# Four equal parts of the channel layer, the first part's weights off GpSimd, and another rate and latency of transfers in the planner

## Chip, cores and metric

One core of one Trainium2 chip runs the whole program. The metric is the device time of one execution in microseconds (us); a measured change of under 0.3%, some 2.4 us, can't be told from none.

## What is computed

Inputs are float32, except U, V, w_ch1, w_ch2, w_in and w_out, which arrive as float64. Three layers follow each other; B = 4, H = 8, S = 576, head width 64, model width 512.

```python
def _attn_ref(q, k, v):                       # per batch and head
    scores = scale * np.matmul(q, k.transpose(0, 1, 3, 2))
    mask = (rel >= 0) & (rel < 128)           # a band of 128 keys
    scores = np.where(mask, scores + bias[None], -1000000000.0)
    attn = softmax(scores)
    return np.matmul(attn, v)

def _moe_ref(x, U, V, w_ch1, w_ch2):
    h = x.transpose(0, 2, 1) @ U @ V          # rank 32, along the sequence
    u = x + h.transpose(0, 2, 1)
    return u + np.maximum(u @ w_ch1, 0.0) @ w_ch2      # 512 -> 2048 -> 512: the channel layer

def _moe2_ref(x, w_in, w_spatial, b_spatial, w_out):
    h = np.maximum(x @ w_in, 0.0)
    u, v = (h[..., :512], h[..., 512:])
    v_n = normalised(v)
    gated = u * (np.einsum('ts,bsd->btd', w_spatial, v_n) + b_spatial)
    return gated @ w_out
```

## The kernel before

Attention runs batch by batch, two heads (a **pair**) at a time, four pairs to a batch. A pair's way (`heads`) is: scores on TensorE (L577), maximum and bias on VectorE (L589, nine tiles), exponential on ScalarE (L594), scaling by the reciprocal sum on VectorE or GpSimd (L607, L609), transposes on TensorE (L616) with copies out (L317, L318), the product with the values (L639). After a batch's fourth pair the rank-32 layer (`low_rank`) multiplies with U (L675) and V (L687) and adds into `u` (L692).

The channel layer's 2048 hidden units are 16 blocks of 128, split into four **parts**; `K["parts"]` says how many blocks each part has. A part's weights stay in SBUF while all 2304 tokens pass (`ffn_group`: first product L460 to L462, ReLU L467 and L469, second product L497 to L499, sum into `y` L507). Every product is three matmuls of operands that are split exactly into a high and a low fp32r part (L431 and L434 for tokens). Part 0 begins early: five groups of 256 tokens (`nb=5`) are interleaved with the attention of batches 1 to 3 and fill TensorE where attention leaves it idle; this is called **filler** below. The other 1024 tokens of part 0 and parts 1 to 3 follow when attention has ended, in groups of 512. The point where the attention ends and 512-wide groups begin is called the **handover** below.

A weight block arrives as float64 and is converted on the chip (`single`, `weights`): load on SP's queue (L350), absolute value on ScalarE (L356), clipping (L360 on GpSimd or L362 on VectorE), and three bit operations on VectorE (L363, L366, L369); then the high part (L317 on ScalarE, or L379 on GpSimd) and the low part on GpSimd (L384). `cp` and `wp` say for how many of part 0's weights the clip and the high part go to GpSimd. V goes the same way without a high and low part; its load (`stacked`) names the 32 rows of V four times, so that the outermost dimension of its source has 4 steps and the next one 32.

The order of the instructions on every engine is set by a planner, `Plan.run`: a list scheduler over the costs, dependences and priorities that each `P.add` gives. `Plan.dma` prices a load at its bytes over a rate, and adds `lat` before its reader may run. Priorities in attention are ten to a pair (`p0 = 10.0 * i`); `low` and `lowd` place V's conversion and its load on that scale, in pairs, `w0` and `w0s` the conversion of part 0's weights, `d0` and `d0s` their loads. On the chip each engine runs its list in order, so what waits for a late load holds up what stands behind it.

Of the kernel before, what the change touches and what calls it, by code (L numbers as in the profile page):

```python
# [126 lines left out]
class Plan:  # L127
# [36 lines left out]

    def dma(self, p, n, emit, r=(), w=(), prio=0):

        self.add("SP", max(0.5, p * n * 4 / 280e3), emit, r=r, w=w, prio=prio, lat=2.3)

    def run(self):
        seq = {t: i for i, t in enumerate(self.tasks)}  # L170
# [89 lines left out]
def tile_kernel(ctx, tc, qT, kT, v, U, V, w1, w2, w_in, wspT, bsp, w_out, bias, out):  # L260
# [32 lines left out]

    r_wa = Ring(in_left, "wa", max(12, 2 * K["parts"][0]))
    r_u = Ring(in_left, "u", 16)
    r_y = Ring(in_left, "y", 12)
    r_raw = Ring(in_left, "raw", 2)
    r_st = Ring(in_left, "st", K["nst"])
    r_h = Ring(in_left, "h", 8)
# [11 lines left out]

    PARTS = K["parts"]

# [10 lines left out]
    def engines(kind, usual):  # L324
        return BOTH if kind in K["flex"] else (usual,)

# [61 lines left out]
    def part_of_hidden(qi, ring, prio, early=lambda c: None, on_pool=lambda c: (False, False)):  # L388
        res = []
        for f in range(PARTS[qi]):  # L390
            c0 = (sum(PARTS[:qi]) + f) * 128
            two = []
            for i, args in enumerate(((block(w1, 0, E, c0, c0 + 128, 4), 4, 128), (block(w2, c0, c0 + 128, 0, E), 1, E))):
                c = 2 * f + i
                two.append(weights(ring, *args, prio(c), early(c), on_pool(c)))
            res.append(two)
        return res
# [142 lines left out]
    def low_rank_weights(prio, early, prio_v, early_v):  # L540
        single(u32, [(0, block(U, 0, 128, 0, RANK)), (1, block(U, 64, S, 0, RANK, 4))], 5, RANK, prio, None, early)
        P.add("DVE", 0.1, lambda: nc.vector.memset(u32[64:, 0], 0.0), w=[u32], prio=prio)
        single(v32, [(0, stacked(block(V, 0, RANK, 0, S), 4))], 1, S, prio_v, None, early_v)
# [152 lines left out]
    for pair in range(4):  # L696
        P.dma(128, 192, lambda pair=pair: nc.sync.dma_start(out=bias_t[:, pair], in_=bias[:, pair]),
              w=[bias_t.part(pair)], prio=20 * pair + 0.5)
    low_rank_weights(15, 2, 10 * K["low"], 10 * K["lowd"])
    parts_w = [None] * 4  # L700
    for b in range(B):
# [7 lines left out]
        if b == 0:  # L709
            parts_w[0] = part_of_hidden(0, r_wa, lambda c: 10 * (K["w0"] + K["w0s"] * c),  # L710
                                        lambda c: 10 * (K["d0"] + K["d0s"] * c),
# [241 lines left out]

K = dict(parts=(5, 4, 4, 3), flex='xeht', cp=3, wp=5, low=4.0, w0=6.5, w0s=1.23, nb=5, evac=40.0, nst=3, d0=5.5, d0s=0.91, lowd=4.1)


# [38 lines left out]
```

## Time and profile before

| | |
|---|---|
| Median of 3 executions | 787.51 us (786.32 to 788.89) |
| The profiled execution | 789.81 us |
| its span, first to last instruction | 788.0 us |
| mean granted TensorE clock | 0.985 |
| TensorE busy | 754.8 us (96%) |
| VectorE, ScalarE, GpSimd busy | 409.6, 319.0, 271.3 us |
| bytes read and written | 40.14 and 4.72 MB |

TensorE is busy for 96% of the span, so what a change is worth is read from the stretches where it is not, and from the stretches where its clock is granted at half. A row of a timeline has start, duration, engine, line, operation, and in brackets the idle time before it with what ended it. A row of a table by groups has the busy time, the mean of one instruction, and the idle time before. PE is TensorE, DVE VectorE, ACT ScalarE, POOL GpSimd, SPq the queue of loads.

### The profile page before, as it was taken

How to read it: one execution, taken by the hardware profiler on the slowest of the kernel's cores; microseconds unless marked ns; L12 is line 12 of the kernel's file. 1: busy time of each engine (PE TensorE's matmuls, PEld its weight loads, DVE VectorE, ACT ScalarE, POOL GpSimd, SP SyncE). 2: the span in 40 equal slices, each digit the busy share in tenths (PEclk: the TensorE clock that was granted, in tenths of full speed). 3: DMA queues.
4: the chain of work that ended last, by engine and by line, in shares of the span. 5: the costliest groups of instructions: out<-in, count | busy, mean ns of one | idle time of the engine just before them, and what ended most of it. 6: DMA issues, size and time to landing. Idle time of an engine off the chain costs nothing.

```text
span 788.0 us, 13153 instructions
## 1 busy us (share of the span) xinstructions
PE 754.8 (96%) x5036; PEld 643.5 (82%) x5036; DVE 409.6 (52%) x1075; ACT 319.0 (40%) x860; POOL 271.3 (34%) x346
## 2 busy tenths in 40 slices
PE   6778799999989999999999999999999999999998
PEld 5557688888888888888887889788998898898887
DVE  4788957587396672212676226822564415325120
ACT  5766657466443442212352115332343332332222
POOL 1364231020173463210474215762436124033021
PEclk9898999999999999999999999999999999999999
DMA  8773213210150350000600003000300100100102
GB/s 218 238 233 115 61 26 102 72 62 17 42 187 1 91 177 1 1 1 0 197 18 0 1 1 108 1 0 1 99 1 1 41 15 0 54 15 1 54 1 67
DMA packets 28834, 45.70 MB, mean 58 GB/s; under 512 B 4964, under 2 KB 18020, under 8 KB 28772
## 3 DMA queue, kind: packets, MB, share of 16 engines
q1 hardware_dynamic: 28772, 44.87, 18.1%
q8 instruction: 39, 0.64, 0.3%
q14 instruction: 23, 0.19, 0.1%
HBM read 40.14 MB, written 4.72 MB: 57 GB/s over the span
## 4 chain that ended last, share of the span: by engine, by line
PE 84%; DVE 9%; DMA 3%; ACT 2%; issue 1%; SPq 0%; DVEq 0%; ACTq 0%
PE at L460 5%; PE at L461 5%; PE at L462 5%; PE sc L499 5%; PE sc L498 5%; PE sc L497 5%; PE at L616 4%; PE acc L497 3%; PE acc L499 3%; PE acc L498 3%; PE at L639 3%; PE f L460 3%; PE sc L779 2%; PE f L461 2%; PE sc L781 2%; PE sc L780 2%
## 5 line engine op out<-in xcount | busy, mean ns | idle before, releaser
L434 POOL TENSOR_TENSOR x<-u,xc 128x64 fp32r<-128x64 f32 (+5 forms) x108 | 91.9, 884 | 126.7 <-ACT xc L431 125.6
L469 DVE SCALAR_TENSOR_TENSOR h<-at,h 128x512 fp32r<-128x512 f32 (+1 forms) x49 | 31.7, 646 | 113.1 <-ACT h L467 113.0
L467 ACT ACTIVATE h<-at 128x512 fp32r<-128x512 f32 (+1 forms) x49 | 27.6, 563 | 122.3 <-PE at L462 121.0
L594 ACT ACTIVATE p<-p,nmax 128x192 f32<-128x192 f32 (+1 forms) x144 | 61.3, 429 | 7.8 <-DVE nmax L589 7.6
L616 PE MATMUL at<-ident,p 128*128 128x128 f32 x272 | 43.4, 309 | 13.9 <-DVE p L609 13.1
L616 PEld LDWEIGHTS at<-ident,p 128*128 128x128 f32 x272 | 35.5, 159 | 20.0 <-issue 11.4
L384 POOL TENSOR_TENSOR wa<-st,wa 128x512 fp32r<-128x512 f32 x26 | 35.0, 1351 | 45.1 <-ACT wa L317 40.2
L589 DVE CUSTOM_DVE_ANT_0 p<-sc,bias 128x192 f32<-128x192 f32 (+1 forms) x144 | 40.2, 328 | 11.9 <-PE sc L577 11.9
L577 PE MATMUL sc<-kr,qr 64*64 64x192 f32 (+2 forms) x576 | 34.5, 341 | 11.2 <-DMA kr<-in_kT 7.4
L497 PE MATMUL acc<-h,wa 128*128 128x256 f32 (+1 forms) x130 | 42.4, 326 | 1.0 <-ACT wb L317 0.9
L794 POOL TENSOR_TENSOR u<-y,u 128x576 fp32r<-128x576 f32 x16 | 23.1, 1460 | 55.0 <-ACT u L792 55.0
L499 PE MATMUL acc<-h,wa 128*128 128x256 f32 (+1 forms) x130 | 40.0, 307 | 2.1 <-DVE h L469 2.1
L498 PE MATMUL acc<-h,wa 128*128 128x256 f32 (+1 forms) x130 | 39.8, 306 | 0.0
L431 ACT CAST xc<-u 128x64 fp32r<-128x64 f32 (+5 forms) x108 | 38.4, 435 | 2.9 <-PE at L687 2.9
L462 PE MATMUL f<-x,wa 128*128 128x256 f32 (+1 forms) x128 | 39.1, 305 | 0.0
L498 PE MATMUL sc<-h,wb 128*128 128x512 f32 (+1 forms) x105 | 38.6, 368 | 0.0
L499 PE MATMUL sc<-h,wb 128*128 128x512 f32 (+1 forms) x105 | 38.6, 368 | 0.0
L497 PE MATMUL sc<-h,wb 128*128 128x512 f32 (+1 forms) x105 | 38.6, 368 | 0.0
L460 PE MATMUL at<-xc,wb 128*128 128x512 f32 (+1 forms) x104 | 38.4, 369 | 0.0
L461 PE MATMUL at<-xc,wb 128*128 128x512 f32 (+1 forms) x104 | 38.3, 369 | 0.0
L462 PE MATMUL at<-x,wb 128*128 128x512 f32 (+1 forms) x104 | 38.3, 369 | 0.0
L317 ACT COPY ph<-at 128x512 f32<-128x512 f32 (+2 forms) x54 | 27.0, 520 | 27.1 <-PE at L616 26.9
(330 smaller groups left out, 2273.2 us busy)
## 6 DMA issues: line engine op xcount, KB each, us to landing
wa<-in_w SPq DMA_DIRECT2D x18, 512.0 KB, 5.3
wb<-in_w SPq DMA_DIRECT2D x14, 512.0 KB, 6.5
qr<-in_qT SPq DMA_DIRECT2D x16, 288.0 KB, 2.9
kr<-in_kT SPq DMA_DIRECT2D x16, 288.0 KB, 3.9
vr<-in_v SPq DMA_DIRECT2D x16, 256.0 KB, 2.8
wa<-in_w_in SPq DMA_DIRECT2D x8, 512.0 KB, 3.5
out<-h SPq DMA_DIRECT2D x15, 256.0 KB, 2.0
wb<-in_w_out SPq DMA_DIRECT2D x4, 512.0 KB, 4.1
```

The lines of the kernel that those rows point to most:

```text
L384: P.add("POOL", pool_tt(k * c), lambda: nc.gpsimd.tensor_tensor(out=b[:, 1], in0=st.ap(), in1=f32(b[:, 0]), op=ALU.subtract), r=[st, b.par ...
L431: nc.scalar.copy(out=th[ih][:, o : o + m], in_=ub[:, s : s + m])
L434: nc.gpsimd.tensor_tensor(out=tl[il][:, o : o + m], in0=ub[:, s : s + m], in1=f32(th[ih][:, o : o + m]), op=ALU.subtract)
L460: nc.tensor.matmul(o, wt[:, 0, k], a[ia], start=k == 0, stop=False)
L461: nc.tensor.matmul(o, wt[:, 1, k], a[ia], start=False, stop=False)
L462: nc.tensor.matmul(o, wt[:, 0, k], l[il], start=False, stop=k == 3)
L497: nc.tensor.matmul(o, wt[:, 0, 0, c], hh[:, j], start=i == 0 and x == 0, stop=False, skip_group_check=True)
L498: nc.tensor.matmul(o, wt[:, 1, 0, c], hh[:, j], start=False, stop=False, skip_group_check=True)
L499: nc.tensor.matmul(o, wt[:, 0, 0, c], hl[:, j], start=False, stop=i == len(wts) - 1, skip_group_check=True)
L589: nc.vector.tensor_tensor_reduce(out=o(), in0=s[:, c0 : c0 + nk], in1=bias_t[:, pair, t % 2, 192 - nk :], scale=-0.125, scalar=BIG, op0=AL ...
L594: nc.scalar.activation(out=o(), in_=o(), func=AF.Exp, scale=-1.0, bias=nmax[:, sl, t : t + 1], accum_out=sums[:, sl, t : t + 1])
L616: P.add("PE", 0.109, lambda pt=pt, t=t, half=half, blk=blk: nc.tensor.transpose(pt[:, blk * 128 : blk * 128 + 128], p[:, t, half * 128 : h ...
```

## The change

```diff
     def dma(self, p, n, emit, r=(), w=(), prio=0):
-        self.add("SP", max(0.5, p * n * 4 / 280e3), emit, r=r, w=w, prio=prio, lat=2.3)
+        self.add("SP", max(0.5, p * n * 4 / 235e3), emit, r=r, w=w, prio=prio, lat=2.6)
...
-K = dict(parts=(5, 4, 4, 3), flex='xeht', cp=3, wp=5, low=4.0, w0=6.5, w0s=1.23, nb=5, evac=40.0, nst=3, d0=5.5, d0s=0.91, lowd=4.1)
+K = dict(parts=(4, 4, 4, 4), flex='xeht', cp=0, wp=0, low=6, w0=8, w0s=1.23, nb=5, evac=40.0, nst=3, d0=7, d0s=0.91, lowd=5)
```

Part 0 has 4 blocks instead of 5 (8 weights to convert instead of 10), the last part 4 instead of 3. None of part 0's weights is clipped or given its high part on GpSimd; the low parts stay there. V's conversion is placed two pairs later, its load almost one, part 0's weights one and a half. The planner believes that a load takes longer. Every engine's list is ordered anew from these costs. Three places follow.

ScalarE's list around the absolute value of V (v_306 and v_365 are V's tile; p_81 and p_77 are the probabilities of odd and even pairs). Before:

```order
L594 ACTIVATE p_81,sums<-p_81,nmax 128x192 x7
L356 ACTIVATE v_306<-raw 128x576
L594 ACTIVATE p_77,sums<-p_77,nmax 128x64
L594 ACTIVATE p_77,sums<-p_77,nmax 128x128
L594 ACTIVATE p_77,sums<-p_77,nmax 128x192 x3
L317 COPY ph<-at 128x384
```

and in the change:

```order
L594 ACTIVATE p_81,sums<-p_81,nmax 128x64
L317 COPY ph<-at 128x256
L594 ACTIVATE p_81,sums<-p_81,nmax 128x128
L594 ACTIVATE p_81,sums<-p_81,nmax 128x192 x7
L594 ACTIVATE p_77,sums<-p_77,nmax 128x64
L594 ACTIVATE p_77,sums<-p_77,nmax 128x128
L594 ACTIVATE p_77,sums<-p_77,nmax 128x192 x7
L317 COPY ph<-at 128x512
L356 ACTIVATE v_365<-raw 128x576
```

V's absolute value stood ahead of all exponentials of batch 0's third pair, and now stands behind them. On SP's queue V's load was the 16th load and the third pair's values followed; now those values go first and V's load is followed by the queries and keys of the fourth pair.

VectorE's list ahead of the scaling (L609) of batch 1's fourth pair (p_81), the last one before that batch's rank-32 layer. Before:

```order
L363 TENSOR_SCALAR st<-st 128x512
L362 TENSOR_SCALAR st<-st 128x512
L366 SCALAR_TENSOR_TENSOR st<-wa,st 128x512
L599 TENSOR_SCALAR rinv<-sums 128x9
L369 SCALAR_TENSOR_TENSOR st<-wa,st 128x512
L601 RECIPROCAL rinv<-rinv 128x9
L363 TENSOR_SCALAR st<-st 128x512
L609 TENSOR_SCALAR p_81<-p_81,rinv 128x64
```

and in the change:

```order
L366 SCALAR_TENSOR_TENSOR st<-wa,st 128x512
L318 COPY ph<-at 128x256
L369 SCALAR_TENSOR_TENSOR st<-wa,st 128x512
L469 SCALAR_TENSOR_TENSOR h<-f_1085,h 128x512
L599 TENSOR_SCALAR rinv<-sums 128x9
L601 RECIPROCAL rinv<-rinv 128x9
L318 COPY u<-at 128x256
L609 TENSOR_SCALAR p_81<-p_81,rinv 128x128
```

Between this pair's first maximum and its scaling the list had eleven operations of weight conversion, and now has two; in batch 0 the conversions were eight operations and are fourteen now, in the whole of batch 1 they were 29 and are 18.

VectorE's list at the handover, from the third of the second four additions of V's product (L692) on. Before:

```order
L692 TENSOR_TENSOR u<-sc,u 128x288
L507 TENSOR_TENSOR y<-acc,u 128x256 x2
L692 TENSOR_TENSOR u<-at,u 128x288
L507 TENSOR_TENSOR y<-acc,u 128x256 x2
L362 TENSOR_SCALAR st<-st 128x512
```

and in the change:

```order
L692 TENSOR_TENSOR u<-sc,u 128x288
L507 TENSOR_TENSOR y<-acc,u 128x128 x4
L692 TENSOR_TENSOR u<-at,u 128x288
L507 TENSOR_TENSOR y<-acc,u 128x128 x4
L362 TENSOR_SCALAR st<-st 128x512
```

Before, these sums belong to the fourth early group, and a fifth one is still under way; now they are the fifth group's, the last. On TensorE 60 early matmuls stood between the last product with V and the first 512-wide one; now 30 do. On GpSimd the twelve token splits of the first two 512-wide groups stood in two blocks of eight and four with two low parts of weights between them; now they stand in one block.

## Rows read from the trace of the kernel before

**Rows 1.** The page, busy time of each engine and its share of the span.
```profile
PE 754.8 (96%) x5036; PEld 643.5 (82%) x5036; DVE 409.6 (52%) x1075; ACT 319.0 (40%) x860; POOL 271.3 (34%) x346
```

**Rows 2.** Busy time by stretches of 20 us; after POOL: granted clock, DMA share, GB/s.
```profile
20.00:40.00 20.00, 14.01 (x146) 10.82 (x138) 14.35 (x65) 14.49 (x52) 7.77 (x9) 0.83 0.79 242
...
80.00:100.00 20.00, 15.65 (x148) 12.88 (x150) 19.97 (x58) 13.45 (x37) 4.84 (x6) 0.91 0.21 61
100.00:120.00 20.00, 20.00 (x238) 17.05 (x235) 10.90 (x44) 9.60 (x35) 6.36 (x11) 1.00 0.16 46
...
220.00:240.00 20.00, 17.92 (x106) 15.91 (x106) 18.70 (x27) 6.68 (x12) 13.04 (x9) 0.91 0.34 121
...
280.00:300.00 20.00, 20.00 (x90) 16.47 (x89) 12.35 (x18) 7.64 (x17) 12.06 (x12) 1.00 0.40 132
```

**Rows 3.** Whom TensorE waited for: us in total, times, longest.
```profile
PE at L616 <- DVE p L609: 13.1, 5, 5.7
PE sc L577 <- DMA kr<-in_kT: 7.4, 2, 4.3
...
PE acc L499 <- DVE h L469: 2.5, 2, 2.1
```

**Rows 4.** The chain of waits, first 30 us: start, duration, what.
```profile
9.45 15.11 DMA raw<-in_V
24.58 0.72 ACT v L356
25.33 0.46 DVE v L362
```

**Rows 5.** The queries' loads, first 70 us: time from issue to landing.
```profile
DMA to landing us min/median/max: 2.8/4.4/14.6
```

**Rows 6.** TensorE's timeline, two transposes of attention and the wait before each.
```profile
26.10 3.86 PE L616 MATMUL at<-ident,p 128*128 128x128 f32 x17 [5.66 <-DVE p L609]
...
94.77 0.82 PE L616 MATMUL at<-ident,p 128*128 128x128 f32 x3 [2.47 <-DVE p L609]
```

**Rows 7.** VectorE, groups by shape, 40 to 108 us.
```profile
L609 DVE TENSOR_SCALAR p<-p,rinv 128x192 f32<-128x192 f32 x29 | 8.6, 363 | 0.0
...
L369 DVE SCALAR_TENSOR_TENSOR st<-wa,st 128x512 uint32<-128x512 uint32 x10 | 8.2, 832 | 0.0
L366 DVE SCALAR_TENSOR_TENSOR st<-wa,st 128x512 uint32<-128x512 uint32 x10 | 7.3, 734 | 0.0
L363 DVE TENSOR_SCALAR st<-st 128x512 uint32<-128x512 uint32 x10 | 5.3, 535 | 0.0
L362 DVE TENSOR_SCALAR st<-st 128x512 f32<-128x512 f32 x7 | 5.1, 738 | 0.0
```

**Rows 8.** VectorE's timeline, conversions in batch 1.
```profile
89.47 1.61 DVE L362 TENSOR_SCALAR st<-st 128x512 f32<-128x512 f32 x1
...
92.17 0.41 DVE L362 TENSOR_SCALAR st<-st 128x512 f32<-128x512 f32 x1
93.22 0.69 DVE L369 SCALAR_TENSOR_TENSOR st<-wa,st 128x512 uint32<-128x512 uint32 x1
```

**Rows 9.** GpSimd, groups by shape, 25 to 108 us.
```profile
L379 POOL TENSOR_TENSOR wa<-st,one 128x512 fp32r<-128x512 f32 x5 | 6.9, 1380 | 10.9 <-DVE st L369 10.9
...
L360 POOL TENSOR_SCALAR st<-st 128x512 f32<-128x512 f32 x3 | 5.7, 1916 | 14.5 <-ACT st L356 14.5
```

**Rows 10.** TensorE's timeline at the handover.
```profile
212.53 0.39 PE L497 MATMUL acc<-h,wa 128*128 128x256 f32 x1
...
219.83 0.39 PE L460 MATMUL at<-xc,wa 128*128 128x512 f32 x1
...
233.61 0.39 PE L499 MATMUL acc<-h,wa 128*128 128x256 f32 x1 [2.08 <-DVE h L469]
```

**Rows 11.** GpSimd's timeline at the handover, the splits of the second 512-wide group.
```profile
228.17 6.19 POOL L434 TENSOR_TENSOR x<-u,xc 128x512 fp32r<-128x512 f32 x4
```

**Rows 12.** VectorE's timeline at the handover, two sums into y.
```profile
213.72 0.75 DVE L507 TENSOR_TENSOR y<-acc,u 128x256 f32<-128x256 f32 x2
```

## The prediction

> **What bounds the kernel now.** The page comes first: TensorE is busy for 96% of the span [rows 1], and where it is full, as at 280 to 300 us, it takes 90 matmuls of 512 columns in 20 us [rows 2]. Time is to be had only where it waits or runs at its lower clock. The second view is the table of stretches: of the sample there, TensorE has 14.0 of 20 us at 20 to 40, 15.7 at 80 to 100, all 20 at 100 to 120 and again 17.9 at 220 to 240. The three stretches with gaps have a granted clock below 1 (0.83, 0.91, 0.91), so part of each ran at 1.2 GHz instead of 2.4. Thus the first 100 us and the handover matter, and nothing else much. The third view says whom TensorE waited for: 13.1 us, in five waits, for VectorE's scaling ahead of the transposes, 7.4 us for keys, 2.5 us for low parts of hidden units [rows 3]. The timeline shows the longest: 5.66 us ahead of 26.10, after which 17 transposes take 3.86 us at the lower clock, and 2.47 us ahead of 94.77 [rows 6]. What held up the first is told by the chain of waits: V's load, issued at 9.45, takes 15.11 us; ScalarE's absolute value and VectorE's clip follow [rows 4], and on both engines the third pair's exponentials and the second pair's scaling stand behind them in the list. Around 90 us the limit is VectorE itself, 19.97 of 20 us busy [rows 2], with weight conversions between the scalings.
>
> **Matmul columns.** Part 0 loses one block: five early groups of 24 matmuls of 256 columns, and two late groups of 24 of 512. The last part gains one: four groups of 24 of 512 and one of 24 of 256. Net, 96 of 256 columns go and 48 of 512 come. Between 212.53 and 219.83 stand 60 of the first kind, 0.122 us each [rows 10]; the second kind is 20/90 = 0.222 us [rows 2]. That is -11.7 + 10.7 = **-1.0 us**, with no doubt about it but rounding, provided that the attention stage really shrinks by what it loses (a rival, below).
>
> **Batch 0, V.** In the change the third pair's exponentials no longer stand behind V's absolute value, and V's clip comes after the second pair's scaling. At most all of the wait of 5.66 us goes, with half of the 3.86 us behind it as the cost of the lower clock, 7.6 us together [rows 6]. At least nothing goes: V's load is not made faster. Against that, batch 0 takes in six more conversions on VectorE, at 0.71 us, the mean of the four conversion rows [rows 7]: 4.3 us. They fill VectorE's waits first. So between -7.6 and +4.3; I take **-1.0 us** at the end of batch 0, since five conversions stand right ahead of the fourth pair's scaling. The Trainium skill bears on the load (DMA: Bandwidth & Descriptors, "Rules for kernel authors"): a source whose outermost dimension has fewer than 16 steps, such as a leading broadcast of c copies, is confined to at most c DMA engines. V's source has 4 there. The rows agree in that 576 KB take 15.11 us [rows 4] where the queries' loads take 4.4 us in the median [rows 5]. By that rule a later place doesn't shorten the load and hurts the loads behind it; what that does to the sum is the second rival.
>
> **Batch 1, VectorE.** Eleven conversions fewer (29 to 18) are -7.8 us at 0.71. By the order, VectorE gets three more scalings there (0.363 us each [rows 7], 1.1 us), two more copies from PSUM (0.7 each, as a 512-wide conversion, 1.4 us), and four sums into `y` (0.75/2 each [rows 12], 1.5 us). Together -3.8 us, on the engine that is full there; the nine conversions that vanish from between the fourth pair's maximum and its scaling are in front of the wait at 94.77. The bounds are 0, if exponentials end last instead, and -7.8.
>
> **Off GpSimd.** Five high parts (6.9 us) and three clips (5.7 us) leave GpSimd [rows 9]. ScalarE gets three casts more and two absolute values fewer, and has slack (13.45 of 20 us [rows 2]). The gain is on VectorE: the same clip takes 1.61 us when GpSimd works beside it and 0.41 alone [rows 8]. If the clean operations cost 0.41 (L362, L363) and 0.69 (L366, L369), the 37 in rows 7 cost 25.9 us instead of 20.8, so all of GpSimd's work there costs 5.1 us. That is one end, zero the other; I take a quarter, **-1.2 us**, as the clips lie before 40 us and the low parts stay.
>
> **Filler in batches 2 and 3.** By the order, 114 early matmuls were through by the end of batch 1, and 120 are now, so nothing is lost there. Between there and the last product with V stood 426, and 330 will: 11.7 us less cover for the scaling chain. TensorE had no gap at 100 to 120 with VectorE busy 10.9 of 20 us [rows 2], so the other engines have room. I allow a few short gaps, **+1.5 us**; the ends are 0 and 11.7.
>
> **Handover.** Before, the only loss was 2.08 us ahead of 233.61 [rows 10] and the lower clock behind it: 0.91 over 20 us [rows 2] is 3.6 us at half, 1.8 us lost, together 3.9. Now 30 matmuls (3.7 us) stand after the last product with V instead of 60, and the last 24 of them need the sum buffer that four additions must first empty, with three of L692 ahead of these; nothing on TensorE covers that: about 1.5 us (two such additions of twice the width took 0.75 us [rows 12]). Then GpSimd's twelve splits run in one block, four of them 6.19 us [rows 11], with six conversions of VectorE beside them at up to 1.6 us ahead of the first low part of hidden units: I put that wait at 2.4 us, and 1.8 us of clock. 5.7 - 3.9 = **+1.8 us**, ends -3.9 and +6. The later joints between parts I take as unchanged, within 1.5 us: their loads are planned more slowly, which can only help a reader that waits, and the last part now needs all eight slots that w_out shared.
>
> **Sum.** -1.0 - 1.0 - 3.8 - 1.2 + 1.5 + 1.8 = -3.7 us. The profiled execution would go from 789.81 to 786.1 us; it lies 2.3 us above the median of the runs, 787.51, from which the same difference gives **783.8 us**. This case alone spans 781.5 to 786.
>
> **Rivals.** *More is gained* (779.8): batch 0 gives 2 us instead of 1, GpSimd's going 2.4 instead of 1.2, and the handover is no worse than before: 4.0 us below the forecast. For it speaks that V's stall is the longest one; against it, that VectorE's list is no shorter over both batches. *V's wait comes back* (789.1): the fourth pair's queries and keys now follow V at once, and its scores stand on TensorE ahead of the second pair's product with the values. If they land as late as before (up to 14.6 us after issue [rows 5]), TensorE stands still there, nothing covers the six conversions, and +4.3 replaces -1.0: +1.6 in all. For it speaks the width of the load; against it, that 512 KB of weights no longer stand between V and these keys. The skill's rule on narrow sources, named above, is this case. *Attention keeps its pace* (794.0): if maximum, exponential and scaling, not TensorE, set the time of batches 2 and 3, the 11.7 us of filler taken out there leave gaps and are paid again after the handover: +10.2 over the forecast's +1.5, net +6.5. It decides from about 6 us of gaps on. Against it speaks the full TensorE at 100 to 120 us with VectorE half idle; for it, that a scaling wait without cover cost 13.1/5 = 2.6 us [rows 3] and there are eight pairs. *It does little*: that a slower rate in the planner only reorders, and the delays cancel, gives 787.5 and counts with the second.
>
> **Chances.** The forecast 0.50 (0.40 of it faster by over 0.3%, 0.10 within), more gained 0.17 (faster), V's wait or little 0.19 (0.16 within, 0.03 slower), attention's pace 0.14 (0.13 slower, 0.01 within). 0.3% is 2.4 us, what a measurement of this kernel can tell. So faster 0.57, same 0.27, slower 0.16. The range 779.5 to 790.5 takes in the first three cases and leaves out most of the last.
>
> **What would show it.** Right: no wait of over 3.5 us ahead of the second pair's transposes; V's load still long, but no engine waiting for it; the last scaling of batch 1 by about 90 us instead of 94; the first 512-wide matmul at about 202 us instead of 219.83 (-14.6 for 120 early matmuls, -6.0, +3.0), with a wait before the last 24 early ones. Wrong: a wait of several us for keys of the fourth pair; repeated gaps ahead of the transposes between 110 and 200 us; more than 6 us of gaps after the last product with V.

## The result, and the profile after

| | before | changed |
|---|---|---|
| Median of 4 executions | 787.49 us | 775.38 us (773.72 to 778.93) |
| Ratio, 95% interval | 1 | 0.9857 (0.9837 to 0.9878) |
| The profiled execution | 789.81 us | 775.38 us |
| its span | 788.0 us | 773.6 us |
| TensorE busy, idle in the span | 754.8, 33.2 us | 748.1, 25.5 us |

The changed kernel is 12.1 us faster by the medians; 3.7 us were forecast. The two spans differ by 14.4 us, since the profiled execution of before lay above its median. Of these, 7.7 us are idle time of TensorE and 6.7 us busy time; 1.0 us of the busy time is the columns; the rest, 5.7 us, is about what the clock gives by the table below (5.0). This page row of the changed kernel answers to [rows 1]:

```profile
PE 748.1 (97%) x4988; PEld 635.7 (82%) x4988; DVE 414.4 (54%) x1077; ACT 317.7 (41%) x856; POOL 263.7 (34%) x344
```

Where it came from is read best by stage. The next two fences are tables of stretches, cut at the last product with V of batch 0, of batch 1 and of batch 3, and at 290 us, by which the handover is over in both kernels. Columns: the stretch, its length, busy time of PE, PEld, DVE, ACT and POOL with instruction counts, TensorE's granted clock, DMA share, GB/s. First the kernel before:

```profile
0.00:49.90 49.90, 34.56 (x400) 27.68 (x400) 31.71 (x141) 29.99 (x102) 15.16 (x32) 0.93 0.78 227
49.90:110.80 60.90, 50.36 (x521) 41.66 (x514) 50.61 (x163) 38.79 (x125) 27.97 (x40) 0.89 0.31 99
110.80:212.20 101.40, 100.66 (x1138) 84.92 (x1130) 67.15 (x288) 59.35 (x216) 12.30 (x28) 1.00 0.17 51
212.20:290.00 77.80, 75.72 (x405) 65.15 (x398) 59.55 (x102) 35.43 (x68) 40.30 (x35) 0.98 0.36 119
```

The same view of the changed kernel:

```profile
0.00:47.30 47.30, 35.53 (x400) 27.56 (x400) 35.79 (x149) 31.63 (x105) 8.98 (x31) 0.89 0.75 233
47.30:99.20 51.90, 46.64 (x528) 38.37 (x520) 44.71 (x159) 34.10 (x117) 18.03 (x28) 0.97 0.41 122
99.20:199.30 100.10, 99.66 (x1134) 84.91 (x1130) 67.68 (x282) 59.66 (x213) 16.37 (x37) 1.00 0.18 52
199.30:290.00 90.70, 86.45 (x396) 70.72 (x389) 69.80 (x107) 39.09 (x79) 53.60 (x49) 1.00 0.29 96
```

Length less busy time is TensorE's idle time, and one less the clock, times the length, bounds what the lower level (1.2 GHz instead of 2.4) cost:

| stage | idle before, after | clock before, after | change | forecast |
|---|---|---|---|---|
| batch 0 | 15.3, 11.8 | 3.5, 5.2 | -1.8 | -1.0 |
| batch 1 | 10.5, 5.3 | 6.7, 1.6 | -10.3 | -5.0 |
| batches 2 and 3 | 0.7, 0.4 | 0, 0 | -0.3 | +1.5 |
| handover to 290 us | 2.1, 4.3 | 1.6, 0 | +0.6 | +1.8 |

With the columns these make 12.8 of the 14.4 us; later idle time (4.5 and 3.8 us) adds 0.7, and 0.9 us are not assigned. The clock's part is a bound, since it counts the lower level in idle time too. The lengths need no bound: batch 0, with the same 400 matmuls, is 2.6 us shorter, and batch 1, with six more early matmuls (0.7 us), 9.0 us. One profile is a coarse measure of the clock. Over all executions its mean is 0.987 before (95 executions, 0.982 to 0.991) and 0.992 after (4): 10.3 and 6.0 us of the span, a gain of 4.3 where the two profiles show 5.0.

The table of waits of the changed kernel (us in total, times, longest) answers to [rows 3]: the waits for the scaling are down from 13.1 to 5.0 us, those for keys hardly, and the sum into `y` is new.

```profile
PE sc L577 <- DMA kr<-in_kT: 6.7, 2, 4.4
PE at L616 <- DVE p L609: 5.0, 6, 2.6
...
PE acc L499 <- DVE h L469: 2.7, 1, 2.7
PE acc L497 <- DVE y L507: 2.0, 2, 1.2
```

**Batch 0.** TensorE's timeline shows 0.82 us ahead of the second pair's transposes, where [rows 6] had 5.66:

```profile
20.21 3.15 PE L616 MATMUL at<-ident,p 128*128 128x128 f32 x17 [0.82 <-POOL p L607]
```

V's absolute value on ScalarE has no idle time before it, so no engine waits for V's load, though its issue at 10.16 is no earlier than in [rows 4]:

```profile
23.33 0.74 ACT L356 ACTIVATE v<-raw 128x576 f32<-128x576 f32 x1
```

**Batch 1.** The fourth pair's scaling on VectorE begins at 84.65, and TensorE's longest wait for a scaling in the batch is 0.9 us:

```profile
84.65 3.05 DVE L609 TENSOR_SCALAR p<-p,rinv 128x128 f32<-128x128 f32 x8
```

The table of waits of this batch alone, before:

```profile
PE at L616 <- DVE p L609: 5.4, 2, 2.9
...
PE f L461 <- POOL wa L384: 0.9, 1, 0.9
```

and in the changed kernel, where no wait for weights is left:

```profile
PE at L616 <- DVE p L609: 1.5, 2, 0.9
```

The waits for the maximum stay (3.2 and 3.3 us). Behind each of the two long waits of before, the stretches show TensorE at the lower level:

```profile
61.60:65.50 3.90, 3.88 (x19) 3.53 (x20) 2.75 (x10) 1.65 (x3) 1.45 (x2) 0.50 0.07 24
...
94.77:98.00 3.23, 3.23 (x16) 3.23 (x17) 3.23 (x8) 0.73 (x2) 1.49 (x2) 0.51 0.00 0
```

In the changed kernel the clock is 1.00 behind the wait of 0.9 us (60.20 to 66.00). VectorE's busy time in the stage is 5.9 us less.

**Batches 2 and 3.** The prediction counted 426 early matmuls between the end of batch 1 and the last product with V before, and 330 now. The groups by shape show 330 in both (three times the counts of L460 and L497). Before:

```profile
L497 PE MATMUL acc<-h,wa 128*128 128x256 f32 x58 | 18.3, 315 | 0.0
...
L460 PE MATMUL f<-x,wa 128*128 128x256 f32 x52 | 15.5, 299 | 0.0
```

and in the changed kernel:

```profile
L460 PE MATMUL f<-x,wa 128*128 128x256 f32 x56 | 16.9, 301 | 0.0
L497 PE MATMUL acc<-h,wa 128*128 128x256 f32 x54 | 16.8, 312 | 0.0
```

The 96 by which the count for the kernel before is too high stood behind the first 512-wide matmul there; the one at 233.61 in [rows 10] is one of them. So no filler was taken out here.

**Handover.** Both forecast waits are in TensorE's timeline, near the sizes forecast (1.5 and 2.4 us). Between them stands the first 512-wide matmul:

```profile
201.89 0.36 PE L497 MATMUL acc<-h,wa 128*128 128x256 f32 x1 [1.23 <-DVE y L507]
...
204.83 0.39 PE L460 MATMUL at<-xc,wa 128*128 128x512 f32 x1
...
213.63 0.50 PE L499 MATMUL acc<-h,wa 128*128 128x512 f32 x1 [2.72 <-DVE h L469]
```

VectorE's timeline shows what stands ahead of the first low part of hidden units (L469), beside GpSimd's block of splits. The four conversions beside the 512-wide splits (from 206.43 on) take 1.48 to 1.77 us; the two that started before, and those in [rows 8] without GpSimd, 0.41 to 0.69:

```profile
205.83 0.45 DVE L362 TENSOR_SCALAR st<-st 128x512 f32<-128x512 f32 x1
206.32 0.43 DVE L363 TENSOR_SCALAR st<-st 128x512 uint32<-128x512 uint32 x1
206.84 1.61 DVE L366 SCALAR_TENSOR_TENSOR st<-wb,st 128x512 uint32<-128x512 uint32 x1
208.37 1.51 DVE L362 TENSOR_SCALAR st<-st 128x512 f32<-128x512 f32 x1
209.81 1.77 DVE L369 SCALAR_TENSOR_TENSOR st<-wb,st 128x512 uint32<-128x512 uint32 x1
211.50 1.48 DVE L363 TENSOR_SCALAR st<-st 128x512 uint32<-128x512 uint32 x1
212.90 0.68 DVE L469 SCALAR_TENSOR_TENSOR h<-at,h 128x512 fp32r<-128x512 f32 x1
```

GpSimd's block, in its timeline:

```profile
200.66 12.03 POOL L434 TENSOR_TENSOR x<-u,xc 128x448 fp32r<-128x448 f32 x12 [0.50 <-ACT xc L431]
```

What the forecast had wrong here is the clock. In short stretches around the wait it stayed at full speed in the changed kernel:

```profile
210.90:213.60 2.70, 0.02 (x1) 0.00 (x0) 2.70 (x4) 1.12 (x2) 2.70 (x3) 1.00 0.95 355
213.60:216.00 2.40, 2.37 (x10) 1.96 (x11) 2.40 (x4) 0.00 (x0) 0.51 (x1) 1.00 0.03 13
```

In the kernel before, a shorter wait was followed by the lower level:

```profile
233.60:236.00 2.40, 2.39 (x10) 2.00 (x11) 2.40 (x2) 0.62 (x1) 2.40 (x2) 0.75 0.00 0
236.00:238.00 2.00, 2.00 (x7) 1.52 (x6) 2.00 (x6) 0.00 (x0) 1.46 (x2) 0.50 0.00 0
```

### The profile page after: what moved, and what is told of

Its sections match the earlier page's. It is cut to its first block, busy times and chain, and to the rows that moved or that the text cites. A ratio compares the mean times of both kernels' runs of the same rounds, so it can differ in the third digit from the quotient of the medians.

```text
span 773.6 us, 13053 instructions
## 1 busy us (share of the span) xinstructions
PE 748.1 (97%) x4988; PEld 635.7 (82%) x4988; DVE 414.4 (54%) x1077; ACT 317.7 (41%) x856; POOL 263.7 (34%) x344
## 4 chain that ended last, share of the span: by engine, by line
PE 87%; DVE 9%; ACT 2%; issue 1%; DMA 1%; SPq 0%; POOL 0%; ACTq 0%; DVEq 0%; POOLq 0%
PE sc L497 5%; PE sc L498 5%; PE sc L499 5%; PE at L460 5%; PE at L461 5%; PE at L462 5%; PE at L616 4%; PE at L639 3%; PE acc L497 3%; PE acc L499 3%; PE acc L498 3%; PE f L460 3%; PE at L780 3%; PE at L779 3%; PE at L781 3%; PE f L461 3%
## 5 line engine op out<-in xcount | busy, mean ns | idle before, releaser
L469 DVE SCALAR_TENSOR_TENSOR h<-at,h 128x512 fp32r<-128x512 f32 (+1 forms) x51 | 32.7, 641 | 96.5 <-ACT h L467 96.5
L616 PE MATMUL at<-ident,p 128*128 128x128 f32 x272 | 41.6, 296 | 6.2 <-DVE p L609 5.0
L460 PE MATMUL at<-xc,wb 128*128 128x512 f32 (+1 forms) x120 | 44.2, 368 | 0.0
L497 PE MATMUL sc<-h,wb 128*128 128x512 f32 (+1 forms) x120 | 44.2, 368 | 0.0
L499 PE MATMUL sc<-h,wb 128*128 128x512 f32 (+1 forms) x120 | 44.1, 368 | 0.0
L498 PE MATMUL sc<-h,wb 128*128 128x512 f32 (+1 forms) x120 | 44.1, 368 | 0.0
L462 PE MATMUL at<-x,wb 128*128 128x512 f32 (+1 forms) x120 | 44.1, 368 | 0.0
L461 PE MATMUL at<-xc,wb 128*128 128x512 f32 (+1 forms) x120 | 44.1, 368 | 0.0
L577 PE MATMUL sc<-kr,qr 64*64 64x192 f32 (+2 forms) x576 | 33.5, 332 | 10.7 <-DMA kr<-in_kT 6.7
L616 PEld LDWEIGHTS at<-ident,p 128*128 128x128 f32 x272 | 33.0, 150 | 12.7 <-issue 4.2
L384 POOL TENSOR_TENSOR wa<-st,wa 128x512 fp32r<-128x512 f32 x24 | 32.6, 1367 | 31.4 <-ACT wa L317 27.8
L384 POOL TENSOR_TENSOR wb<-st,wb 128x512 fp32r<-128x512 f32 x20 | 30.9, 1555 | 31.3 <-ACT wb L317 31.3
L469 DVE SCALAR_TENSOR_TENSOR h<-f,h 128x512 fp32r<-128x512 f32 (+1 forms) x27 | 17.8, 658 | 43.0 <-ACT h L467 42.9
L467 ACT ACTIVATE h<-f 128x512 fp32r<-128x512 f32 (+1 forms) x27 | 15.4, 571 | 53.2 <-PE f L462 52.1
L497 PE MATMUL acc<-h,wa 128*128 128x256 f32 (+1 forms) x108 | 35.6, 329 | 1.5 <-DVE y L507 1.2
L577 PEld LDWEIGHTS sc<-kr,qr 64*64 64x64 f32 x576 | 21.8, 141 | 17.5 <-issue 10.1
```

Of the source, the lines that this page charges most:

```text
L384: P.add("POOL", pool_tt(k * c), lambda: nc.gpsimd.tensor_tensor(out=b[:, 1], in0=st.ap(), in1=f32(b[:, 0]), op=ALU.subtract), r=[st, b.par ...
L460: nc.tensor.matmul(o, wt[:, 0, k], a[ia], start=k == 0, stop=False)
L461: nc.tensor.matmul(o, wt[:, 1, k], a[ia], start=False, stop=False)
L462: nc.tensor.matmul(o, wt[:, 0, k], l[il], start=False, stop=k == 3)
L469: P.add("DVE", dve(per * n), lambda f1=f1, hh=hh, hl=hl: nc.vector.scalar_tensor_tensor(out=hl.ap(), in0=f1.ap(), scalar=0.0, in1=f32(hh.a ...
L497: nc.tensor.matmul(o, wt[:, 0, 0, c], hh[:, j], start=i == 0 and x == 0, stop=False, skip_group_check=True)
```

## Experiments: each setting alone and undone

My theory after the result was that V's place gives the gain in batch 0 and fewer conversions on VectorE that in batch 1. The rivals: the planner's price of a load moves everything, or the order is a matter of luck. Five kernels make one part of the change in the kernel before, and five undo one in the changed kernel.

```diff
alone, in the kernel before:
  e2_rate    280e3 -> 235e3, lat 2.3 -> 2.6
  e3_pool    cp=3, wp=5 -> cp=0, wp=0
  e4_parts   parts (5, 4, 4, 3) -> (4, 4, 4, 4)
  e5_v_late  low 4.0 -> 6, lowd 4.1 -> 5
  e6_w_late  w0 6.5 -> 8, d0 5.5 -> 7
undone, in the changed kernel:
  f1_rate, f2_pool, f3_parts, f4_v_early, f5_w_early: the same lines back
```

> The kernel before with the planner's other price of a load alone (235 instead of 280, 2.6 instead of 2.3). If the price is a small part of the change, the time is 785 to 790 and the wait ahead of the second pair's transposes is still 4 us or more. Rival: the price alone moves the loads so that the first pairs' data come sooner, and gives half of the gain or more: 777 to 782.

> The kernel before with cp=0 and wp=0 alone: three clips and five high parts leave GpSimd. If GpSimd's work beside VectorE's conversions cost most of what was lost in batch 1, the last scaling of batch 1 is at about 90 us instead of 94.2 and the time is 782 to 784. Rival: it costs about a quarter of that, as predicted (1.2 us), or is eaten by the clips that VectorE gets: 785.5 to 788.

> The kernel before with four equal parts alone: two conversions fewer in batches 0 and 1, 1.0 us of matmul columns less, 120 of 600 early matmuls gone. If batch 1 is bound by the number of conversions on VectorE, the time is 783 to 785.5. Rival: the filler that is gone is missed in batches 2 and 3 and at the handover: gaps there of 3 us or more, time 788 to 793.

> The kernel before with V's load and conversion placed later alone (lowd 4.1 to 5, low 4.0 to 6). If the order around V is what gives the gain in batch 0, the wait of 5.66 us ahead of the second pair's transposes falls below 3.5 us, batch 0 ends at least 2.5 us before 49.8, and the time falls by 2.5 to 6 us, to 780 to 784. Rival: the wait only moves to the keys that now follow V on the queue, and the time is within 1.5 us of 786.3.

> The kernel before with the loads and the conversion of part 0's weights placed one and a half pairs later alone (d0 5.5 to 7, w0 6.5 to 8). If VectorE's full stretch in batch 1 comes from where these conversions stand, batch 1 ends 3 us or more before 110.8 (the last product with V of the batch) and the time is 781 to 784. Rival: the conversions are only pushed on, the early matmuls start later and TensorE has less to do in its gaps: batch 1 ends no sooner, time 786 to 791.

> The changed kernel with the planner's old price of a load alone put back (280 and 2.3). If the price carries its own share of the gain (3.3 us when changed alone), the time is 778 to 781 and the transposes of the second pair start later than 20.2 by 1 us or more. Rival: the price is worth nothing once the weights are placed late, and the time stays within 1.5 us of 775.4.

> The changed kernel with cp=3 and wp=5 alone put back: three clips and five high parts on GpSimd again. Changed alone this was worth nothing (786.4 beside 786.3). If that holds here too, the time is 774 to 777. Rival: with the weights placed late these operations fall beside the scalings of batch 1 and delay them: batch 1 ends 2 us or more after 99.2, time 778 to 783.

> The changed kernel with the old parts (5, 4, 4, 3) alone put back. If fewer conversions in batch 1 carry the gain, the time goes back to 780 or more and batch 1 ends 3 us or more later than 99.2. Rival: since four equal parts alone added 8 us to the kernel before, they are no help here either, and the time is at or below 775.4 (770 to 776).

> The changed kernel with V's load and conversion put back to their old places (lowd 4.1, low 4.0) alone. If V's later place carries the gain in batch 0, the second pair's transposes start at 23 us or later instead of 20.2, batch 0 ends at 49.5 or later instead of 47.3, and the time is 778 to 782. Rival: the planner's new price of a load already moves V out of the way, and the time stays within 1.5 us of 775.4.

> The changed kernel with part 0's weights put back to their old places alone (d0 5.5, w0 6.5). Changed alone the later place cost 2.5 us, through waits at the handover, while batch 1 ended 8.9 us sooner. If it is this later place that frees batch 1 in the change, and four blocks in place of five that keep the handover from paying it back, the time is 780 or more and batch 1 ends 3 us or more after 99.2. Rival: the place is a loss here too, and the time is 770 to 775.

Measured, as ratios to the kernel before with their 95% intervals. The last column is the step in us that making the setting brings in the company of the other four: 787 times (0.9857 less the ratio undone), uncertain by some 2.5 us.

| setting | alone | us | undone | made in company, us |
|---|---|---|---|---|
| price of a load | 0.9950 (0.9934 to 0.9967) | -3.9 | 1.0042 (1.0024 to 1.0060) | -14.6 |
| off GpSimd | 1.0005 (0.9986 to 1.0024) | +0.4 | 0.9920 (0.9898 to 0.9942) | -5.0 |
| four equal parts | 1.0112 (1.0084 to 1.0140) | +8.8 | 0.9916 (0.9886 to 0.9946) | -4.6 |
| V later | 1.0020 (0.9998 to 1.0043) | +1.6 | 0.9872 (0.9841 to 0.9902) | -1.2 |
| weights later | 1.0031 (1.0010 to 1.0052) | +2.4 | 0.9985 (0.9964 to 1.0007) | -10.1 |

Alone they add up to +9.3 us; together they give -11.3. A term per setting, each with a price of its own, can't describe this change. V's later place is worth nothing that can be measured, against my theory. The price of a load, which I had counted under "it only reorders", is the largest step. The weights' later place loses alone, as much as its rival said though batch 1 ends 8.9 us sooner there, and is worth 10 us in company. Of the other expectations, e3_pool, e5_v_late and f4_v_early came out as their rivals had it, f2_pool's time as its rival had it, though batch 1 ended only 0.9 us later, and f5_w_early as expected; e2_rate and f3_parts lie between the two, and e4_parts and f1_rate are slower than either.

Most of what four equal parts lose alone shows at the handover of e4_parts, where TensorE idles for 7.4 us up to 290 us instead of 2.1. Its timeline there:

```profile
228.59 0.80 PE L499 MATMUL acc<-h,wa 128*128 128x512 f32 x1 [5.41 <-DVE h L469]
```

On VectorE eight conversions instead of six stand ahead of this L469, again beside a block of twelve splits (12.02 us). The clock falls within the empty stretch and stays low behind it:

```profile
223.20:228.60 5.40, 0.01 (x1) 0.01 (x1) 5.40 (x6) 1.12 (x2) 3.85 (x3) 0.77 0.63 228
228.60:231.00 2.40, 2.40 (x6) 1.94 (x7) 2.40 (x4) 0.62 (x1) 1.08 (x1) 0.50 0.00 0
```

With the old price put back into the changed kernel (f1_rate) the same eight conversions stand there, and the wait is 4.7 us. So one part of the price's effect is seen (6.7 us of idle time at that handover against 4.3 in the changed kernel, and a clock of 0.50 behind the wait): with the dearer load the planner puts two of part 1's conversions behind the low part that TensorE waits for.

## Experiments: V's load

Here every list of the kernel before (e1_v_four) or of the changed one (g1_v_four) is kept, and V comes in four loads.

```diff
-                nc.sync.dma_start(out=..., in_=src)
+                for g in range(4):
+                    nc.sync.dma_start(out=o[32 * g : 32 * g + 32]..., in_=src[g])
```

> The kernel before, with its lists of every engine unchanged, but V is loaded by four loads of 32 rows each instead of one load with a source of 4 x 32 steps. If V's slow load is what holds up the second pair, it lands within 7 us instead of 15.1, the wait of 5.66 us ahead of the second pair's transposes falls below 1.5 us, and the time falls by 3 to 7 us, to 780.5 to 784.5. Rival: the lists of ScalarE and VectorE hold it up and the load is only the last to be seen: the wait stays over 3.5 us, and the time is within 1.5 us of 787.5.

Measured 780.67 us, ratio 0.9943 (0.9916 to 0.9970): 4.5 us faster, as expected. The four loads are a row of the page:

```profile
raw<-in_V SPq DMA_DIRECT2D x4, 144.0 KB, 4.4
```

They land 4.4 us after issue in the median, where the one load took 15.11 [rows 4], and the second pair's transposes wait 2.12 us instead of 5.66 (a little more than expected). This kernel's file is a few lines longer, so that L620 and L613 are L616 and L609 here:

```profile
19.45 2.19 PE L620 MATMUL at<-ident,p 128*128 128x128 f32 x17 [2.12 <-DVE p L613]
```

The Trainium skill's rule that was weighed in the prediction (DMA: Bandwidth & Descriptors, "Rules for kernel authors") says that a source with an outermost dimension of fewer than 16 steps uses no more engines than it has steps. The runs agree: with 32 steps in place of 4, a quarter of the bytes takes 0.29 of the time with three others under way. How many engines moved them, no view shows.

> The changed kernel with V loaded by four loads of 32 rows. In the kernel before this took 8 us from batch 0. If V's slow load still holds back the loads behind it here, batch 0 ends 3 us or more before 47.3 and the time is 768 to 773. Rival: by its later place V is out of everyone's way already, and the time stays within 1.5 us of 775.4.

Measured 774.08 us, ratio 0.9849 (0.9823 to 0.9875): the same as the changed kernel, as the rival said. ScalarE takes up V at 23.19 us, though the four loads were issued by 12.3 us and took at most 4.5 to land; its place in the list decides. So in the change's order V's slow load holds up nothing.

## Experiments: what sets batch 1

h1_less_dve takes half of part 0's conversion work off VectorE in the kernel before, with every list kept.

```diff
-        P.add("DVE", dve(n), lambda: nc.vector.scalar_tensor_tensor(   # L366 and L369
+        P.add("DVE", dve(n), lambda: None if bits_out else nc.vector.scalar_tensor_tensor(
```

> The kernel before, every list as it was, but of the conversion of part 0's ten weights the two VectorE operations that merge the words (20 operations of about 0.75 us, 15 us on VectorE, some 10 of them in batch 1) are left out. If the amount of conversion work on VectorE sets batch 1, its scaling waits go (the 2.9 and 2.5 us ahead of the transposes of batch 1 fall below 1 us), the idle time of TensorE in batch 1 falls from 10.5 to about 5.5 us as in the change, the half-clock time with it, and the time falls by 5 to 9 us, to 778 to 782. Rival: it is the place of the conversions and of the loads, not their amount; the idle time in batch 1 stays over 8.5 us and the time falls by less than 3 us.

Measured 785.0 us, ratio 0.9978 (0.9963 to 0.9994): 1.7 us. The stage of batch 1:

```profile
50.90:108.30 57.40, 48.13 (x518) 38.92 (x514) 41.51 (x148) 37.09 (x124) 25.11 (x36) 0.94 0.34 106
```

VectorE has 9.1 us less to do there than before, and TensorE's idle time goes from 10.5 to 9.3 us only. The long waits for the scaling are cut (2.9 to 1.7 at most), but there are five of them instead of two. The stage is 3.5 us shorter, and batch 0 is 1.0 us longer in this profile. In the old order the amount of conversion thus counts for some of the change's 9.0 us in batch 1, and not for the larger part. The weights come hardly sooner for it, the last low part at 102.0 us instead of 104.5: here are the low parts of part 0's weights on GpSimd (L384), minimum, median and maximum duration in ns, first and last start. Before, then the changed kernel:

```profile
L384 POOL TENSOR_TENSOR wa<-st,wa x10: 1266/1274/1537, 49.1 to 104.5; 128x512 fp32r<-128x512 f32 x10
```
```profile
L384 POOL TENSOR_TENSOR wa<-st,wa x8: 1262/1286/1371, 35.6 to 84.8; 128x512 fp32r<-128x512 f32 x8
```

In the changed kernel the last weight is ready some 39 us after batch 0's end, before it took 56 us. Early matmuls can't run before their weights, and while attention waits TensorE has nothing else to run. That became the next theory. The test lets the early matmuls use the first block for every block, in the kernel before and in f1_rate; all else is still loaded and converted. The planner makes new lists for both, so their gains hold a change of order too.

```diff
-        ffn_group(g * 256, 256, parts_w[0], 1e4 + g, True, K["evac"], True)
+        ffn_group(g * 256, 256, parts_w[0][:1] * PARTS[0], 1e4 + g, True, K["evac"], True)
```

> The kernel before, where the early matmuls of part 0 use the first block's weights for every block, so that they need wait for two weights instead of ten; all ten are still loaded and converted. If batch 1 is set by the moment at which weights are ready for the early matmuls, more than the 114 of before are through by the end of batch 1, the idle time there falls from 10.5 to 5.5 us or less, and the time falls by 4 to 9 us, to 778 to 783. Rival: attention's own chain and VectorE set it: the idle time stays over 8.5 us, the time within 2.5 us of 786.9.

> The changed kernel with the planner's old price of a load (789.5 us) and with the early matmuls on the first block's weights for every block. If the price worked through the readiness of the weights, the idle time of batch 1 falls from 10.7 to 6 us or less and the time by 5 us or more, to 784 or less; what is left over the 775.4 of the changed kernel is the handover (5 us more waiting and clock in the trace with the old price). Rival: the price works elsewhere, and the time stays at 787 to 791.

i1_one_block: 780.11 us, ratio 0.9917 (0.9897 to 0.9937), 6.5 us faster than before, inside the expected span. Batch 1:

```profile
48.00:106.70 58.70, 51.24 (x564) 43.13 (x556) 49.91 (x169) 39.06 (x126) 29.97 (x42) 0.97 0.34 105
```

Early matmuls through by the end of batch 1 are 156 instead of 114 (three times the counts of L460 and L497, the groups by shape up to that end). Before:

```profile
L460 PE MATMUL f<-x,wa 128*128 128x256 f32 x28 | 9.0, 323 | 0.0
...
L497 PE MATMUL acc<-h,wa 128*128 128x256 f32 x10 | 3.6, 358 | 0.0
```

and i1_one_block:

```profile
L460 PE MATMUL f<-x,wa 128*128 128x256 f32 x32 | 10.1, 317 | 1.2 <-DVE h L469 1.2
...
L497 PE MATMUL acc<-h,wa 128*128 128x256 f32 x20 | 6.3, 313 | 0.0
```

TensorE's idle time is 7.5 us, between the two expectations, and the clock 0.97 as in the changed kernel. i2_one_block_price: 785.49 us, ratio 0.9979 (0.9967 to 0.9991), 5.0 us better than f1_rate by the ratios but over the 784 expected. Batch 1 there and, below it, in f1_rate:

```profile
47.10:105.10 58.00, 53.29 (x575) 44.35 (x568) 47.01 (x159) 35.49 (x119) 23.35 (x37) 0.97 0.36 111
```
```profile
47.40:104.40 57.00, 46.26 (x488) 36.66 (x484) 48.08 (x167) 35.63 (x121) 17.95 (x25) 0.91 0.37 114
```

Idle time falls from 10.7 to 4.7 us as expected; the handover takes some back (8.4 us idle up to 290, 6.7 in f1_rate). So freeing the early matmuls of their weights gives 6.5 and 5.0 us, and lifts the clock; by the measure of the stage table batch 1 gives 7.9 and 9.4 us, where the change had 10.3. That is what sooner filler can give. That it is what the change gave is not shown: only 120 early matmuls are through by the end of batch 1 in the changed kernel, 114 before. What speaks for it is their place, 24 instead of 12 ahead of the first wait for a scaling in the batch. Against it, e3_pool began its last low part at 96.2 us instead of 104.5, had 8.2 us idle in batch 1, and gained no time, and h3_rate200 (below) has 84 through and 6.3 us idle.

## Experiments: more from the price, and the handover

> The changed kernel with a still dearer load in the planner (200 and 2.95 in place of 235 and 2.6, a step as large again as the change's). If a dearer load keeps readers of late data from holding up their engines, the time is no worse than 777 and may fall to 770. Rival: the gain of the price is luck of one order out of many: the time is as likely anywhere between 775 and 790, and over 780 would say so.

h3_rate200 (200e3 and 2.95 in the changed kernel): 778.89 us, ratio 0.9906 (0.9887 to 0.9925). It lies above the 777 expected and below the 780 that would have spoken for luck, so it decides nothing between the two, but a still dearer load doesn't help: it is 3.9 us slower than the change.

h2_first puts the first L469 three conversions earlier on VectorE; h5_first_four does so in g1_v_four.

```diff
+        t = self.first[0]            # the first L469 of the 512-wide groups
+        i = [x for x in order if x.eng == "DVE"]
+        at = order.index(i[i.index(t) - 3])
...
+        order[at:] = [x for x in rest if x in up] + [x for x in rest if x not in up]
```

> The changed kernel, where the first low part of hidden units of the 512-wide groups is put three operations earlier on VectorE, ahead of three conversions that take 4.8 us beside GpSimd's block (all other lists the same, but for one absolute value on ScalarE). If those three make the wait of 2.72 us, it falls below 0.5 us and the time by 2 to 3 us, to 772.5 to 773.5. Rival: the wait only moves to the next low part or to the next weight that is converted later: time within 1 us of 775.4.

> The changed kernel with both: V in four loads and the first low part of hidden units three operations earlier. If both add up, 774.1 less 2 to 3 us: 771 to 772.5. Rival: one of them eats the other, 773.5 to 775.5.

h2_first: 777.15 us, ratio 0.9887 (0.9868 to 0.9905); h5_first_four: 776.0 us, 0.9864 (0.9843 to 0.9885). Neither gains; the rivals were right. VectorE's timeline of h2_first (L480 and L512 are L469 and L499 there) shows the first low part at 210.04, in time, and the second behind five conversions, three of which take 1.5 to 1.8 us beside GpSimd:

```profile
210.04 0.69 DVE L480 SCALAR_TENSOR_TENSOR h<-at,h 128x512 fp32r<-128x512 f32 x1
...
216.59 0.68 DVE L480 SCALAR_TENSOR_TENSOR h<-at,h 128x512 fp32r<-128x512 f32 x1
```

TensorE now waits for that one, 0.7 us less than in the changed kernel:

```profile
217.32 0.50 PE L512 MATMUL acc<-h,wa 128*128 128x512 f32 x1 [2.02 <-DVE h L480]
```

But behind this shorter wait the clock falls, as it did not in the changed kernel, and that takes the gain back:

```profile
217.30:220.00 2.70, 2.68 (x7) 2.17 (x8) 2.63 (x4) 1.21 (x2) 1.34 (x1) 0.59 0.00 0
```

Nothing that ran is faster than the changed kernel by more than the runs can tell; g1_v_four, f4_v_early and h5_first_four can't be told from it.

## Why the prediction was wrong

**The step that failed** is the term "Batch 1, VectorE", -3.8 us with -1.2 beside it. It priced the work taken off VectorE, in VectorE's own time, and put the lower clock at nothing. VectorE's time was sized well (5.9 us less in the stage), and TensorE's idle time did fall by about the sum (5.3 us). But the granted clock in the batch also rose from 0.89 to 0.97, worth up to 5.1 us more, because the waits of 2.9 and 2.5 us went that had the lower level behind them; the stage became 9.0 us shorter instead of 5.0. The prediction used the price of the lower clock in batch 0's bounds and at the handover, and not here, though [rows 2] had 0.91 at 80 to 100 us.

That idle time fell by the sum forecast is in part luck. Taking 9.1 us off VectorE in the old order (h1_less_dve) cuts it by 1.2 us only, and the kernel's time by 1.7, while freeing the early matmuls of their weights (i1_one_block) cuts it by 3.0 and the time by 6.5. VectorE being full at 80 to 100 us [rows 2] was right, but it is not the only limit; when filler is ready is another, which the prediction didn't price. How the change's gain divides between them is not shown.

**Batch 0, V.** Taken at -1.0 with bounds of -7.6 and +4.3; measured -1.8 by the table and -2.6 by the length of the stage. The wait of 5.66 us went, VectorE's six more conversions did fit in, and the lower clock took 1.0 to 1.7 us back. The reason given, V's later place, is not shown: f4_v_early puts V back and loses 1.2 us, within the uncertainty.

**Off GpSimd.** A quarter of 5.1 us was taken. In company it is 5.0, uncertain by some 2.5, the outer end; alone it is nothing.

**Filler, +1.5.** Not paid, since the term rests on a wrong count: 330 early matmuls, not 426, stood in batches 2 and 3, and 330 do now. No cover was taken away, so the 0.4 us idle there say nothing of the room that other engines had.

**Handover, +1.8.** The two waits came as sized. The 1.8 us for the clock did not; in e4_parts (a wait of 5.41 us) and in h2_first (2.02 us) the clock fell.

**Rivals.** "More is gained" was the right direction and too small. "V's wait comes back" had a true premise, the narrow load is worth 4.5 us in the kernel before (e1_v_four), but in the change's order no engine waits for it. "Attention keeps its pace" rests on the same wrong count as the filler: its 11.7 us were never taken out, so it was not put to the test. "It does little" treated the price of a load as a reorder without effect; it gives 3.9 us alone and 14.6 in company.

**Signs.** The last scaling of batch 1 was expected by 90 us and begins at 84.65; the first 512-wide matmul at 202 and stands at 204.83, between the two waits forecast. That it comes so near is luck: of the 120 early matmuls that were to leave the stretch ahead of it (-14.6 us) only 24 did, 504 to 480, which is 2.9 us; batches 0 and 1 gave 11.6 us in their place, where 6.0 were forecast.

**Open.** Why the price of a load is worth so much in company is shown for the handover and in part for batch 1, no further. Which order the planner finds for another price can't be told from these runs, and that part of the gain is the luck of one order is not ruled out.

## What to carry to other kernels

Price a gap in TensorE's work with the lower clock that stands behind it, wherever the table of stretches shows a clock below 1, and not only where the gap is long; take the price as a bound, for at the handover it did not come. When a planner makes the order, test settings together and undo them one at a time: four equal parts cost 8.8 us alone and are worth 4.6 in company. Where independent work fills another stage's gaps, ask when its inputs are ready, and not only how busy the engine is that prepares them; and count from the trace how much of it stands in the stage.

## What the runs showed of the hardware

A wait of 2.08 us at the handover of the kernel before was followed by the lower clock level, and so was one of 2.02 us in h2_first; one of 2.72 us in the changed kernel was not, nor were those of 2.69 in g1_v_four and 2.71 in f2_pool, in the same place. The length of the gap alone doesn't tell.

Conversions on VectorE beside GpSimd's 512-wide splits (four of them, 1.6 us each on average) take 1.5 to 1.8 us instead of 0.4 to 0.7, while L469, which reads PSUM, takes 0.7 beside them (at 210.04 in h2_first) or alone. The Trainium skill (SBUF — State Buffer, "SBUF: two separate sides") has a reason for such a step: VectorE, in a two-port mode or with two inputs from SBUF, and GpSimd take a shared pair of ports for a whole instruction, and the other waits. The trace agrees in size: the extra time, 0.9 to 1.1 us, is less than one such split.
